# Reading an exchanged buffer back in halves, on alternate partitions and earlier

## The chip, the core and the metric

The kernel runs on one core of one Trainium2 chip. The metric is the device time of one execution in microseconds (us), lower is better. A run is "fast" or "slow" (a slow run shows a lower granted TensorE clock, or is more than 1.5% above the fastest run of the same kernel).

## The reference

Two frequency-domain filters of one input are mixed by a gate (cut to what matters; the second filter has the same form):

```python
def filt(x, w_r, w_i):                       # x: 1 x 2048 x 1024, bf16
    X = jnp.fft.rfft2(x.astype(jnp.float32), axes=(-2, -1))
    X = X * (w_r + 1j * w_i)
    return jnp.fft.irfft2(X, s=(2048, 1024), axes=(-2, -1)).astype(jnp.bfloat16)

g = sigmoid((x * gate_w).sum(-1, keepdims=True))
return g * filt(x, A_w_r, A_w_i) + (1 - g) * filt(x, B_w_r, B_w_i)
```

## The kernel before

All transforms are matmuls. The middle of the kernel goes through 16 **units** of rows, 8 for the even columns and 8 for the odd ones. Each unit is multiplied by the weights and given a first inverse transform; the result has to change its layout, so it is stored to a scratch tensor in DRAM and read back in 8 **parts** per parity. A part then gets its second inverse (L564), its third (L580 and L589), and the sums of even and odd results that make the output.

The whole program is one list of tokens. Each engine takes its own tokens in that order, and all the DMAs concerned are issued from SyncE, one in-order queue: in SyncE's timelines they come in the order of the list. The tokens that matter here:

```python
ORDER = """ ...
... EX:0:0:A H:11:1 L:0:5 VC:0:1:0:A EQ:0:0:0:P ...
... VC:0:2:1:D V:0:5:0:6 L:0:6 C:0:2:0:7 EQ:3:0:0:P L:0:7 ...
... L:1:0 EX:5:0:D C:0:4:1:6 L:1:1 EQ:3:1:0:P EX:5:1:A L:1:2 L:1:3 ...
... """
# J first inverse of a unit   R its copy out of PSUM   H its store to scratch
# L:parity:part  read-back    V second inverse         VC its copy
# C, U third inverse          EX copy of an even result for GpSimd
# EQ:part:s:h:P  one even sum on GpSimd     OC OP OR QD QP  odd sums     S store of the output
# GW gate weights   W, c loads of weights and constants   P weight product
```

The tiles and the functions that the argument touches:

```python
Re = big.tile([P, NS1 * 1024], BF16, name="re")      # even read-back (and, earlier, the input)
Ro = big.tile([P, NS1 * 1024], BF16, name="ro")      # odd read-back
y  = big.tile([P, 2, 2, 2, 2 * NT, NS1, 4], BF16, name="y")
RR = [r[:].rearrange("p (v r s f) -> p v r s f", v=8, r=2, s=2) for r in (Re, Ro)]
EV = Re[:].bitcast(F32).rearrange("p (v s f) -> p v s f", s=2, v=8)   # even sums, in the bytes of Re
# ... cut ...
def exchange_row(t, i):
    return 8 * t + 4 * (i % 2) + i // 2

def scratch_store(n, tt, q="S"):
    a = 4 * (n % NU) + 2 * tt
    Q[q].dma_start(SC[n // NU][a:a + 2].rearrange("a p m -> p a m"), RLs[n][:, tt])

def scratch_load(par, v, q="S"):
    Q[q].dma_start((Re, Ro)[par][:, v * 2048:v * 2048 + 2048],
                   SC[par][:].rearrange("a (h v q) m -> (a h) v (q m)", h=4, v=8)[:, v])

def even_mix(v, s, h, e):
    t = TM["X", v, s]
    Q[e].tensor_tensor(EV[:, v, s, 256 * h:256 * h + 256], t[:, 0], t[:, 1], (ALU.add, ALU.subtract)[h])

def store(q, v, s="b"):
    r = slice(0, 2) if s == "b" else slice(int(s), int(s) + 1)
    Q[q].dma_start(ov[:, 2 * v:2 * v + 2, :][:, r], OT[v][:, r].rearrange("p s h d -> p s (h d)"))
```

One line will matter more than it seems to: `EV`, the place of the even sums, is the tile `Re` under another type. The sums of part v go into exactly the bytes that the read-back of part v had filled, after these were used. Nobody writes waits by hand: a layer records which tile region each instruction reads and writes, and puts the semaphore waits into the built program.

## Time and profile before

| | before |
|---|---|
| time, median of 3 runs | 116.65 us (115.95 to 117.53) |
| the profiled execution | 117.98 us, span 116.2 us |
| TensorE, VectorE, ScalarE, GpSimd busy | 88%, 83%, 74%, 40% |
| last unit's matmuls end | 78.26 us |
| first odd second-inverse group starts | 90.31 us |
| GpSimd's even sums start | 74.86 us |

The profiled execution was 1.3 us longer than the median. Spans of single profiled executions therefore carry a spread of a microsecond or two; ratios come from the timed rounds.

Three views of the end. First, two rows of the stretches table (window, length, then busy us and count of TensorE, its weight loads, VectorE, ScalarE, GpSimd, then granted clock, DMA share, GB/s):

```profile
85.00:90.00 5.00, 4.05 (x52) 3.32 (x51) 1.69 (x3) 3.15 (x6) 5.00 (x8) 1.00 0.78 246
90.00:95.00 5.00, 5.00 (x59) 3.76 (x57) 3.09 (x6) 2.86 (x6) 4.53 (x7) 1.00 1.02 405
```

TensorE is four fifths busy in the first and full in the second; GpSimd is full. Next, SyncE's timeline (start, length, line, operation, out<-in, count), which shows when loads are issued:

```profile
80.66 1.31 SPq L553 DMA_DIRECT2D re<-sc  x2
85.01 5.63 SPq L553 DMA_DIRECT2D ro<-sc  x7
```

The last two even loads need 1.31 us of the queue, and seven of the eight odd loads follow from 85.01. Last, the row of the odd read-back tile (shortest/mean/longest ns, then from when to when):

```profile
L564 PE MATMUL ps<-ea,ro x64: 219/219/220, 90.3 to 108.2; 128*128 128x128 bf16 x64
```

### The profile page before, as it was taken

What the parts mean: (1) busy time and instruction counts of PE and PEld (TensorE: products, weight loads), DVE (VectorE), ACT (ScalarE), POOL (GpSimd) and SP (SyncE); (2) the same over time, 40 slices, a digit from 0 to 9 for tenths busy, and PEclk for the clock granted to TensorE, in tenths of its full rate; (3) what the DMA queues carried; (4) which work ended last, traced back from release to release, by engine and by line L of the source; (5) the groups of instructions that cost most, each with busy time, mean ns of one, the idle gap of its engine ahead of it and who ended that gap; (6) DMA issues with size and microseconds to landing.
All of it is one profiled execution on the core that took longest, in us unless ns stands there. A gap on an engine that the chain in (4) does not pass through costs nothing.

```text
span 116.2 us, 3965 instructions
## 1 busy us (share of the span) xinstructions
PE 101.9 (88%) x1619; PEld 69.5 (60%) x1619; DVE 96.0 (83%) x161; ACT 85.8 (74%) x142; POOL 46.2 (40%) x72
## 2 busy tenths in 40 slices
...
GB/s 88 295 344 406 413 367 318 367 402 393 95 202 349 367 394 393 350 395 353 254 328 302 256 281 395 379 378 379 339 266 278 402 409 148 309 261 392 80 337 205
DMA packets 17794, 36.79 MB, mean 317 GB/s; under 512 B 1904, under 2 KB 10736, under 8 KB 17776
## 3 DMA queue, kind: packets, MB, share of 16 engines
...
q14 instruction: 6, 0.05, 0.1%
...
## 4 chain that ended last, share of the span: by engine, by line
DMA 33%; PE 29%; ACT 19%; DVE 7%; SPq 4%; issue 4%; DVEq 1%; ACTq 0%
DMA re<-sc 9%; PE ps L564 9%; ACT rl L203 8%; PE ps L580 7%; DMA wj<-cst_wj 7%; DMA re<-in_x_dram 7%; DMA ro<-in_we_dram 6%; PE ps L589 5%; ACT X L203 4%; PE ps L536 4%; DMA sc<-rl 4%; ACT T L203 4%; DVE p L493 3%; DVE ot L634 3%; PE ps L449 2%
## 5 line engine op out<-in xcount | busy, mean ns | idle before, releaser
L614 POOL TENSOR_TENSOR re<-wx 128x256 f32<-128x256 f32 x24 | 17.1, 739 | 55.1 <-DMA sc<-rl 50.5
L203 ACT CAST rl<-ps 128x1024 bf16<-128x1024 f32 x28 | 28.9, 1170 | 0.2 <-PE ps L536 0.2
L203 ACT COPY wx<-ps 128x256 f32<-128x256 f32 (+1 forms) x42 | 17.8, 481 | 10.0 <-PE ps L333 6.7
L381 DVE TENSOR_TENSOR y<-ps,wx 128x256 bf16<-128x256 f32 x48 | 16.4, 412 | 7.9 <-ACT wx L203 7.8
L203 ACT CAST V<-ps 128x512 bf16<-128x512 f32 x21 | 12.3, 611 | 11.5 <-PE ps L564 8.6
L536 PE MATMUL ps<-p,wj 32*64 32x512 bf16 x512 | 19.2, 381 | 1.0 <-ACT rl L203 0.5
L493 DVE TENSOR_TENSOR p<-X,ro 128x2048 bf16<-128x2048 bf16 x16 | 18.9, 1216 | 0.0
L449 PE MATMUL ps<-fd,y 128*128 128x256 bf16 x128 | 17.3, 273 | 0.3 <-ACT ea L433 0.3
L333 PE MATMUL ps<-f,re 128*128 128x128 bf16 x256 | 15.6, 220 | 1.5 <-DMA re<-in_x_dram 1.2
L333 PEld LDWEIGHTS <-re 128*128 128x128 bf16 x256 | 14.7, 98 | 3.0 <-DMA re<-in_x_dram 2.3
L203 ACT CAST T<-ps 128x512 bf16<-128x512 f32 x26 | 16.0, 687 | 0.0
L203 ACT CAST X<-ps 128x1024 bf16<-128x1024 f32 x14 | 15.8, 1126 | 0.1
L634 DVE TENSOR_TENSOR ot<-re,ps 128x512 bf16<-128x512 f32 x20 | 12.4, 678 | 1.9 <-issue 1.9
L449 PEld LDWEIGHTS <-y 128*128 128x128 bf16 x128 | 11.1, 97 | 4.5 <-issue 3.5
L536 PEld LDWEIGHTS <-wj 32*64 32x64 bf16 x512 | 8.4, 103 | 8.1 <-issue 5.0
L381 POOL TENSOR_TENSOR y<-wx 128x256 bf16<-128x256 f32 x16 | 11.1, 736 | 5.2 <-ACT wx L203 5.2
L580 PE MATMUL ps<-ig,V 128*128 128x512 bf16 x48 | 11.5, 380 | 0.3 <-ACT V L203 0.3
L479 PE MATMUL ps<-T,wf 64*64 64x512 bf16 (+1 forms) x128 | 10.5, 333 | 1.0 <-ACT X L203 0.4
L589 PE MATMUL ps<-ig,V 128*128 128x256 bf16 x80 | 10.5, 273 | 0.3 <-ACT V L203 0.3
L205 DVE CAST V<-ps 128x512 bf16<-128x512 f32 x11 | 7.4, 683 | 3.9 <-PE ps L564 3.9
L564 PE MATMUL ps<-ea,re 128*128 128x128 bf16 x64 | 8.3, 220 | 1.9 <-DMA re<-sc 1.6
L646 POOL TENSOR_TENSOR ot<-pq 128x512 bf16<-128x512 f32 x8 | 9.9, 1268 | 0.2 <-POOL re L614 0.2
...
## 6 DMA issues: line engine op xcount, KB each, us to landing
...
```

Of the source, the lines that this page charges most:

```text
L203: nc.scalar.copy(out=out, in_=in_)
L333: nc.tensor.matmul(o, lhsT=lh, rhs=rh, start=(h == 0), stop=(h == 1))
L381: Q[e].tensor_tensor(yo[:, v, k:k + n, s1, :], a.rearrange("p (k c) -> p k c", c=4), b.rearrange("p (k c) -> p k c", c=4), op)
L449: nc.tensor.matmul(ps[:, v * 256:v * 256 + 256], lhsT=y[:, v, par, b, 2 * t:2 * t + 2, :, :].rearrange("p j s c -> p (j s c)"), rhs=C["FD" ...
L479: nc.tensor.matmul(view(ps[ho, tt * 512:(tt + 1) * 512], dst), lhsT=lh, rhs=view(T[hp(jh), tt, :], src), start=(w == 0), stop=(w == 1))
L493: nc.vector.tensor_tensor(p[:, r], xb, w, ALU.mult)
L536: nc.tensor.matmul(o, lhsT=lh, rhs=src[r, ri, wi, tt], start=(q == 0), stop=(q == 3))
L564: nc.tensor.matmul(ps[:, ch * 128:ch * 128 + 128], lhsT=RR[par][:, v, ch // 2, s, c0 + 256 * ab:c0 + 256 * ab + 128], rhs=Ew[:, s1, :], st ...
L580: nc.tensor.matmul(ps, lhsT=Vs[par, v][:, s, ch, :], rhs=rh, start=(ch == 0), stop=(ch == 3))
L589: nc.tensor.matmul(ps[:, o:o + 256], lhsT=Vs[par, v][:, s, ch, :], rhs=g[:, o:o + 256], start=(ch % 2 == 0), stop=(ch % 2 == 1))
L614: Q[e].tensor_tensor(EV[:, v, s, 256 * h:256 * h + 256], t[:, 0], t[:, 1], (ALU.add, ALU.subtract)[h])
L634: nc.vector.tensor_tensor(otile(v)[:, s, h, :], EV[:, v, s], PS["O", 1, v, s], (ALU.add, ALU.subtract)[h])
```

## The change

The intent: let the read-back of a parity begin when half of its units are stored. Each load is cut in two: half g = 0 takes the scratch rows of the parity's first four units, half g = 1 those of the other four. The rows are permuted (in `exchange_row`, through the constants) so that a half lands on every second partition instead of on 64 adjacent ones. The list of tokens was arranged anew around this, with first halves ahead of the stores of later units, and the last two output stores are cut in halves. The core of the diff (most of the list, the unpacking of arguments and a load of a constant in two pieces are cut):

```diff
 def exchange_row(t, i):
-    return 8 * t + 4 * (i % 2) + i // 2
+    r = 8 * t + 4 * (i % 2) + i // 2
+    return 2 * (r % 64) + r // 64
@@
-    def scratch_load(par, v, q="S"):
-        Q[q].dma_start((Re, Ro)[par][:, v * 2048:v * 2048 + 2048],
-                       SC[par][:].rearrange("a (h v q) m -> (a h) v (q m)", h=4, v=8)[:, v])
+    def scratch_load(par, v, g, q="S"):
+        Q[q].dma_start((Re, Ro)[par][g:P:2, v * 2048:v * 2048 + 2048],
+                       SC[par][16 * g:16 * g + 16].rearrange("a (h v q) m -> (a h) v (q m)", h=4, v=8)[:, v])
@@
-    def store(q, v, s="b"):
+    def store(q, v, s="b", h="b"):
@@
+        if h == "b":
+            Q[q].dma_start(o.rearrange("p s h d -> p s (h d)"), OT[v][:, r].rearrange("p s h d -> p s (h d)"))
+        else:
+            Q[q].dma_start(o[:, :, int(h)], OT[v][:, r, int(h)])
@@ ORDER, the stretch that matters
+... C:0:1:0:7 EX:1:1:A V:0:0:1:4 R:14:0:A R:14:1:D EQ:1:1:0:P ... EQ:1:1:1:P H:14:1 J:15:2:0
+... EX:0:1:D C:0:3:0:3 H:15:1 V:0:2:0:0 L:0:6:1 EX:3:1:D EQ:0:1:0:P V:0:5:1:1 L:0:7:0 ...
+C:0:2:1:2 EQ:3:1:0:P L:0:7:1 EX:3:0:D V:0:5:0:6 L:1:0:0 EQ:0:1:1:P C:0:2:0:0 L:1:1:0 ...
```

More of the change, by code (lines that the diff above doesn't have):

```diff
@@ L24 @@
 ORDER = """
-warm:8 c:A:F1 c:A:gws tab:A x:S:0:1 x:S:1:1 x:S:2:2 x:S:4:2 x:S:6:2 x:S:8:2 x:S:10:2 x:S:12:2 x:S:14:2 gc:P c:S:FD:0:1
-F1:1:o:0 F1:0:o:1 F1:1:e:2 F1:0:e:3 FC:1:e:A F1:3:e:4 FD:1:e FC:0:e:A F1:3:o:5 FD:0:e F1:2:e:6 FX:3:o:A FC:2:e:A
-FP:3:o FX:0:o:A F1:5:e:5 FD:2:e FC:3:e:A F1:4:e:7 FD:3:e F1:5:o:1 FC:4:e:A FP:0:o F1:4:o:6 FC:5:e:A F1:7:e:4 FD:5:e
-F1:6:e:2 FD:4:e FC:7:e:A c:S:WF:0:4 F1:9:e:3 FC:6:e:A W:S:0 F1:8:e:5 FD:6:e FC:9:e:A F1:2:o:7 FX:1:o:A FD:9:e
-c:S:WJ:0:4 F1:10:e:2 FX:4:o:A FP:1:o F1:11:e:0 FD:7:e c:S:w0 FC:8:e:A F1:6:o:3 c:S:PM FD:8:e FC:11:e:A F1:7:o:4 c:S:EZ
@@ L30 @@
-FC:10:e:A FP:4:o FX:6:o:A FD:11:e F1:12:e:6 W:S:1 F1:13:e:5 FD:10:e FC:12:e:A c:S:WF:4:16 F1:15:e:0 FX:2:o:A FP:6:o
-FD:12:e F1:14:e:3 FC:13:e:A FC:15:e:A W:S:2 F1:12:o:2 FD:13:e F1:8:o:6 FP:2:o FC:12:o:A FD:15:e F1:11:o:7 FC:14:e:A
-FX:5:o:A c:S:WJ:4:16 F1:10:o:5 FD:14:e FC:8:o:A F1:13:o:0 FP:5:o FC:10:o:A FD:12:o F1:15:o:1 neg:A:0:4 FX:7:o:A
-F2:0:0:3 FD:10:o c:S:E FC:11:o:A F2:1:1:2 W:S:3 FC:13:o:A FP:7:o FD:11:o T:0:0:A F1:9:o:4 F2:0:1:5 FC:15:o:A FD:8:o
-W:S:4 FC:9:o:A F2:1:0:3 T:0:1:A pw:P FD:13:o F1:14:o:7 T:1:0:A F3:0:5 FD:15:o c:S:FD:1:2 FC:14:o:A F2:2:1:0 X:0:A
@@ L35 @@
-T:1:1:D W:S:5 F2:2:0:3 FD:9:o F3:1:1 neg:A:4:16 F2:3:0:5 FD:14:o W:S:6 T:2:0:A F2:3:1:4 P:0:0 T:3:0:A Y:0:6 GH:3 X:1:A
-NA:0:D P:0:1 T:2:1:A T:3:1:A F3:2:0 N:0:D GC:A P:1:0 J:0:4:6 X:2:A F2:4:0:2 P:1:1 R:0:0:A Y:1:3 F2:4:1:0 GT:0:1 NA:1:D
-R:0:1:A T:4:0:D F3:3:4 Y:2:3 P:2:0 GT:2:1 T:4:1:A H:0:1 F2:5:0:2 W:S:7 X:3:A GT:3:1 c:S:IG GT:1:1 N:1:D P:2:1 F2:5:1:0
-T:5:0:A F3:4:4 GK:A T:5:1:A W:S:8 J:1:6:1 NA:2:D P:3:0 X:4:A H:0:0 F2:6:0:0 R:1:0:A W:S:9 P:3:1 F3:5:4 F2:6:1:3
-R:1:1:A H:1:0 Y:4:6 Y:3:7 P:4:0 X:5:A H:1:1 GZ:0:1 W:S:10 P:4:1 GS:0 GZ:1:4 NA:3:D GS:1 N:2:D F2:7:1:1 NA:4:D GW:D:0
@@ L40 @@
-F2:7:0:2 N:3:D J:2:6:4 N:4:D T:7:0:D T:7:1:A T:6:0:A W:S:11 T:6:1:A GW:D:4 R:2:0:A J:3:0:2 P:5:0 R:2:1:A H:2:0 F3:6:6
-P:5:1 R:3:0:A Y:5:4 F2:8:0:5 X:6:D R:3:1:A H:3:0 F3:7:0 W:S:12 H:2:1 T:8:0:A NA:5:D P:6:0 J:4:2:6 W:S:13 X:7:A P:6:1
-R:4:0:A Y:7:0 Y:6:1 F2:9:1:4 F2:8:1:5 R:4:1:A H:4:0 N:5:D NA:6:D NA:7:D W:S:14 F2:9:0:2 P:7:0 H:3:1 T:8:1:A J:5:0:6
-T:9:0:A P:7:1 T:9:1:A F3:8:2 R:5:0:A F2:10:1:5 N:7:D X:8:D F2:10:0:4 R:5:1:A H:5:0 F3:9:0 H:4:1 T:10:0:A T:10:1:D
-H:5:1 J:7:2:6 X:9:A N:6:D P:8:0 R:7:0:A J:6:4:0 P:8:1 R:7:1:A F2:11:1:2 F2:11:0:3 R:6:0:A R:6:1:D H:7:1 F3:10:6 P:9:0
@@ L45 @@
-T:11:0:A H:6:1 J:8:0:4 H:6:0 X:10:A H:7:0 T:11:1:D F2:12:0:3 R:8:0:A P:9:1 F3:11:6 R:8:1:A F2:12:1:2 H:8:0 T:12:0:D
-X:11:A H:8:1 J:9:0:4 P:10:0 W:S:15 T:12:1:A P:10:1 R:9:0:A F3:12:2 F2:13:1:6 R:9:1:A H:9:0 F2:13:0:7 P:11:0 T:13:0:A
-H:9:1 J:10:0:4 L:0:0 P:11:1 X:12:A L:0:1 L:0:2 T:13:1:A P:12:0 R:10:0:A F3:13:2 F2:15:0:6 R:10:1:D X:13:A H:10:0
-F2:14:1:7 L:0:3 F2:14:0:0 L:0:4 T:15:0:A P:12:1 J:11:2:4 T:14:0:A T:14:1:A P:13:0 R:11:0:A J:12:0:6 P:13:1 R:11:1:A
-F3:14:2 X:14:A V:0:0:0:4 F2:15:1:5 R:12:0:A R:12:1:D P:14:0 H:12:1 J:13:2:6 T:15:1:A H:12:0 H:10:1 VC:0:0:0:A P:14:1
@@ L50 @@
-F3:15:0 V:0:0:1:5 V:0:1:0:4 R:13:0:D R:13:1:A X:15:A H:13:1 C:0:0:0:6 V:0:1:1:7 VC:0:0:1:A P:15:0 H:13:0 J:14:0:2
-EX:0:0:A H:11:1 L:0:5 VC:0:1:0:A EQ:0:0:0:P VC:0:1:1:D R:14:0:A C:0:1:0:6 P:15:1 C:0:0:1:4 R:14:1:A C:0:1:1:5
-V:0:3:0:7 GW:D:8 EX:1:0:A H:14:1 J:15:0:2 H:14:0 EX:1:1:D VC:0:3:0:A H:11:0 GW:D:12 V:0:3:1:6 EQ:1:1:0:P R:15:0:A
-V:0:2:1:5 VC:0:3:1:D V:0:2:0:7 R:15:1:A H:15:0 EQ:0:0:1:P C:0:3:0:0 VC:0:2:0:D C:0:3:1:1 EQ:1:1:1:P EX:3:0:A H:15:1
-VC:0:2:1:D V:0:5:0:6 L:0:6 C:0:2:0:7 EQ:3:0:0:P L:0:7 EX:3:1:D C:0:2:1:0 VC:0:5:0:D EQ:1:0:0:P V:0:4:0:5 V:0:5:1:1
@@ L55 @@
-EQ:3:0:1:P VC:0:4:0:D V:0:4:1:6 VC:0:5:1:A EQ:1:0:1:P C:0:4:0:5 EX:0:1:A C:0:5:0:1 VC:0:4:1:A EQ:0:1:0:P C:0:5:1:4
-L:1:0 EX:5:0:D C:0:4:1:6 L:1:1 EQ:3:1:0:P EX:5:1:A L:1:2 L:1:3 V:0:6:1:1 EX:4:0:A EQ:3:1:1:P L:1:4 V:0:6:0:4 EX:4:1:A
-L:1:5 EQ:5:1:0:P L:1:6 VC:0:6:0:A VC:0:6:1:D V:0:7:1:5 EQ:5:1:1:P C:0:6:1:1 EQ:4:0:0:P V:0:7:0:4 C:0:6:0:6 EQ:0:1:1:P
-VC:0:7:0:D VC:0:7:1:A C:0:7:1:5 E:6:1:D V:1:0:0:2 EQ:4:1:0:P V:1:0:1:3 EX:7:1:D VC:1:0:0:A EQ:5:0:0:P C:0:7:0:1
-E:2:1:A VC:1:0:1:D U:1:0:0:2 EQ:7:1:0:P EQ:7:1:1:P V:1:1:0:0 U:1:0:1:3 EQ:5:0:1:P VC:1:1:0:A OC:0:0:A V:1:2:1:4
@@ L60 @@
-EQ:4:0:1:P E:2:0:A V:1:2:0:0 OP:0:0:0 OR:0:1:1 EX:7:0:A OR:0:1:0 U:1:1:0:2 VC:1:2:0:A VC:1:2:1:D V:1:1:1:1 E:6:0:A
-EQ:4:1:1:P OR:1:0:0 C:1:2:0:0 VC:1:1:1:A C:1:2:1:3 OP:0:0:1 QD:2:0:0 U:1:1:1:1 QD:2:1:0 EQ:7:0:0:P S:S:0 V:1:3:0:4
-L:1:7 QD:2:1:1 V:1:3:1:5 QP:2:0:0:P VC:1:3:0:A QD:2:0:1 V:1:4:0:6 VC:1:3:1:A OR:1:1:1 V:1:4:1:3 VC:1:4:0:A U:1:3:0:0
-QP:2:1:0:P OR:1:0:1 OR:1:1:0 U:1:3:1:4 VC:1:4:1:D QP:2:0:1:P S:S:1 U:1:4:0:1 OR:3:0:0 OR:3:1:0 U:1:4:1:5 QP:2:1:1:P
-OC:4:0:A OR:3:1:1 V:1:6:0:2 V:1:6:1:1 OP:4:0:0 OR:4:1:1 S:S:2 VC:1:6:0:A V:1:5:0:3 OR:3:0:1 VC:1:6:1:A C:1:6:0:2
@@ L65 @@
-OR:4:1:0 S:S:3 VC:1:5:0:A OP:4:0:1 C:1:6:1:4 QD:6:0:0 V:1:5:1:0 QD:6:1:0 U:1:5:0:1 VC:1:5:1:A EQ:7:0:1:P S:S:4
-QD:6:0:1 U:1:5:1:0 QP:6:0:0:P QD:6:1:1 OR:5:0:0 V:1:7:0:5 V:1:7:1:4 QP:6:1:0:P OR:5:0:1 VC:1:7:0:A VC:1:7:1:A OR:5:1:0
-U:1:7:0:5 OR:5:1:1 QP:6:1:1:P U:1:7:1:1 OR:7:0:0 S:S:5 OR:7:0:1 QP:6:0:1:P OR:7:1:1 S:S:7:0 OR:7:1:0 S:S:6 S:S:7:1
+warm:8 c:A:F1 tab:A x:S:0:1 x:S:1:1 x:S:2:2 x:S:4:2 x:S:6:2 x:S:8:2 x:S:10:2 x:S:12:2 x:S:14:2
+c:S:FD:0:1 F1:0:e:0 F1:1:e:1 FC:0:e:D F1:1:o:2 FC:1:e:A FD:0:e FD:1:e F1:3:e:3 F1:2:e:0 FC:3:e:A F1:3:o:1
@@ new lines @@
+FC:2:e:A F1:2:o:4 FD:2:e FX:3:o:A F1:4:e:5 FX:2:o:A FP:3:o F1:4:o:0 FX:1:o:A FC:4:e:D F1:5:o:1 FD:3:e
+F1:5:e:2 FP:2:o FD:4:e F1:6:e:4 FC:5:e:A F1:7:e:3 FX:5:o:A FD:5:e c:S:WF:0:4 F1:9:e:5 FC:7:e:A FP:1:o
+W:S:0 FC:6:e:A F1:8:e:1 FD:7:e FC:9:e:A F1:6:o:2 FC:8:e:A FD:9:e F1:7:o:6 c:S:WJ:0:4 FP:5:o FX:4:o:A
+F1:11:e:3 FD:8:e c:S:w0 FX:6:o:A F1:10:e:0 c:S:PM FD:6:e FC:11:e:A F1:0:o:1 c:S:gws FP:6:o FC:10:e:A
+FD:11:e F1:12:e:2 c:S:EZ F1:13:e:7 FD:10:e FC:12:e:A F1:14:e:3 FP:4:o FC:13:e:A FD:12:e FX:7:o:A F1:15:e:4
@@ new lines @@
+F1:9:o:0 FC:14:e:A FD:13:e F1:13:o:2 W:S:1 FP:7:o FC:9:o:A FD:14:e F1:15:o:5 c:S:WF:4:16 FC:15:e:A FC:13:o:A
+F1:11:o:6 FD:15:e FX:0:o:A F1:14:o:3 FC:11:o:A FD:9:o W:S:2 F1:8:o:1 FC:15:o:A gc:P neg:A:0:4 c:S:WJ:4:16
+F2:1:0:4 FD:13:o FC:14:o:A FC:8:o:A F2:1:1:0 c:S:E T:1:0:A FD:15:o F1:10:o:7 pw:P W:S:3 T:1:1:A
+F2:0:0:2 FD:11:o FC:10:o:A F3:1:4 T:0:0:A FD:8:o W:S:4 F1:12:o:0 X:1:A FD:14:o F2:0:1:2 F2:3:1:1
+FP:0:o FD:10:o FC:12:o:A c:S:FD:1:2 Y:1:3 T:0:1:A F2:3:0:6 FD:12:o W:S:5 neg:A:4:16 F3:0:4 NA:1:D
@@ new lines @@
+P:1:0 F2:2:0:2 T:3:0:A F2:2:1:0 X:0:A W:S:6 GH:3 P:1:1 T:2:0:A T:2:1:A W:S:7 N:1:D
+T:3:1:A P:0:0 GC:A c:S:IG P:0:1 F3:2:4 F3:3:0 X:2:A F2:5:0:2 Y:0:3 T:5:0:A J:1:6:4
+NA:0:D X:3:A P:2:0 F2:5:1:2 R:1:0:A Y:3:3 P:2:1 Y:2:0 F2:4:0:1 T:5:1:A H:1:0 GT:0:6
+T:4:0:A F2:4:1:7 NA:3:D W:S:8 N:0:D NA:2:D N:2:D R:1:1:A P:3:0 J:0:2:0 T:4:1:A H:1:1
+GT:2:6 P:3:1 R:0:0:A W:S:9 F3:4:4 GT:1:6 X:4:A R:0:1:D GT:3:6 F3:5:2 F2:6:0:7 GK:A
+X:5:A P:4:0 GZ:1:4 H:0:1 F2:7:1:6 H:0:0 GS:1 J:2:0:2 W:S:10 N:3:D P:4:1 T:6:0:A
@@ new lines @@
+GW:P:8 Y:4:4 F2:7:0:5 R:2:0:D R:2:1:A T:7:0:A GZ:0:2 NA:4:D T:7:1:A H:2:0 P:5:0 J:3:0:4
+GS:0 Y:5:6 F2:6:1:7 R:3:0:A N:4:D GW:D:4 T:6:1:A P:5:1 F3:7:2 H:3:0 X:7:A H:2:1
+F3:6:0 NA:5:D N:5:D X:6:A P:7:0 J:4:6:2 R:3:1:A F2:8:0:0 P:6:0 Y:7:1 R:4:0:A H:3:1
+Y:6:4 F2:8:1:5 W:S:11 NA:6:D NA:7:D P:6:1 T:8:0:A F2:9:0:4 H:4:0 T:8:1:A W:S:12 J:5:6:0
+R:4:1:A P:7:1 F2:9:1:5 R:5:0:A H:4:1 F3:8:2 T:9:0:D T:9:1:A X:8:D H:5:0 R:5:1:A W:S:13
+F3:9:4 F2:10:0:6 N:7:D N:6:D X:9:A P:8:0 H:5:1 J:7:0:2 L:0:0:0 T:10:0:A GW:D:0 R:7:0:A
@@ new lines @@
+J:6:4:6 P:8:1 R:7:1:A F2:10:1:0 F2:11:0:1 R:6:0:A R:6:1:D F2:11:1:2 T:11:0:A P:9:0 H:6:1 J:8:4:6
+T:10:1:A H:7:1 T:11:1:A H:6:0 F3:10:0 P:9:1 H:7:0 F2:12:1:2 W:S:14 R:8:0:D R:8:1:A X:10:A
+L:0:1:0 F3:11:6 L:0:2:0 F2:13:1:3 X:11:A H:8:1 F2:12:0:0 P:10:0 F2:13:0:1 T:12:0:A J:9:4:6 H:8:0
+P:11:0 T:13:0:A T:12:1:A T:13:1:A P:10:1 F3:12:0 R:9:0:A F2:14:0:2 F2:14:1:3 P:11:1 X:12:A H:9:0
+F3:13:4 L:0:3:0 T:14:0:D T:14:1:A W:S:15 R:9:1:A L:0:0:1 P:12:0 J:10:0:2 L:0:1:1 X:13:A H:9:1
+P:12:1 L:0:2:1 R:10:0:A J:11:6:4 L:0:3:1 P:13:0 R:10:1:A F3:14:0 L:0:4:1 R:11:0:D X:14:A H:10:1
@@ new lines @@
+F2:15:0:2 F2:15:1:3 R:11:1:A J:12:0:6 H:10:0 T:15:0:A T:15:1:D P:13:1 L:0:4:0 V:0:0:0:3 R:12:0:A V:0:1:1:2
+L:0:5:1 P:14:0 V:0:1:0:4 R:12:1:A H:11:1 F3:15:0 H:11:0 VC:0:1:0:A VC:0:1:1:D P:14:1 X:15:A L:0:5:0
+J:13:6:4 H:12:0 VC:0:0:0:A P:15:0 R:13:0:A L:0:6:0 J:14:0:2 H:12:1 P:15:1 R:13:1:A C:0:1:1:6 H:13:0
+C:0:1:0:7 EX:1:1:A V:0:0:1:4 R:14:0:A R:14:1:D EQ:1:1:0:P V:0:3:0:5 V:0:3:1:6 VC:0:3:0:D EQ:1:1:1:P H:14:1 J:15:2:0
+VC:0:3:1:A H:14:0 GW:D:12 VC:0:0:1:A H:13:1 C:0:0:0:5 R:15:0:A C:0:0:1:4 R:15:1:D C:0:3:1:6 H:15:0 V:0:2:1:2
@@ new lines @@
+EX:0:1:D C:0:3:0:3 H:15:1 V:0:2:0:0 L:0:6:1 EX:3:1:D EQ:0:1:0:P V:0:5:1:1 L:0:7:0 VC:0:2:0:D VC:0:2:1:A EX:0:0:A
+C:0:2:1:2 EQ:3:1:0:P L:0:7:1 EX:3:0:D V:0:5:0:6 L:1:0:0 EQ:0:1:1:P C:0:2:0:0 L:1:1:0 VC:0:5:0:D VC:0:5:1:A V:0:4:0:1
+EQ:3:1:1:P V:0:4:1:3 VC:0:4:0:D EQ:0:0:0:P C:0:5:1:6 VC:0:4:1:A EX:1:0:D C:0:4:0:1 EQ:3:0:0:P EX:5:1:A L:1:0:1 C:0:4:1:3
+EX:4:0:A EQ:5:1:0:P L:1:1:1 V:0:6:1:4 L:1:2:0 V:0:6:0:1 EQ:4:0:0:P L:1:2:1 C:0:5:0:5 EQ:0:0:1:P L:1:3:1 V:0:7:0:6
+VC:0:6:0:D VC:0:6:1:A E:2:0:A L:1:4:1 C:0:6:1:4 EQ:4:0:1:P VC:0:7:0:D L:1:5:1 V:0:7:1:7 EQ:3:0:1:P EX:4:1:D C:0:6:0:0
```

18 lines of the change are left out of this document (16 added, 2 removed).

## The prediction

> **What bounds the kernel now.** I read the page first, for shares; then the stretches table (busy time per engine, granted clock, DMA share, GB/s in windows), to cut the run into stages; then the chain that ended last, to see which wait decides each stage; then the timelines of the vector engine and GpSimd over the end.
>
> The page's first row only says that nothing is idle and nothing is full:
>
> ```profile
> PE 101.9 (88%) x1619; PEld 69.5 (60%) x1619; DVE 96.0 (83%) x161; ACT 85.8 (74%) x142; POOL 46.2 (40%) x72
> ```
>
> The stretches table gives each stage its own limit (columns: window, length, then busy us and count of PE, PEld, DVE, ACT, POOL, then clock, DMA share, GB/s):
>
> ```profile
> 50.00:72.00 22.00, 20.38 (x396) 11.18 (x393) 21.79 (x23) 22.00 (x30) 0.00 (x0) 1.00 0.96 316
> 78.00:88.00 10.00, 8.36 (x120) 6.83 (x104) 6.21 (x11) 5.68 (x10) 8.17 (x12) 1.00 0.95 327
> 100.00:106.00 6.00, 6.00 (x57) 4.01 (x56) 6.00 (x11) 2.25 (x6) 6.00 (x6) 1.00 0.75 293
> ```
>
> The reader is to see three regimes. From about 26 to 80 us (the middle row set stands for it), ScalarE and VectorE are both full: they evacuate PSUM and multiply by the weights, GpSimd does nothing, and TensorE follows. From 78 to 88 neither is full. From 94 on VectorE, GpSimd and TensorE are full together. The gap in the second stretch is explained by the chain (start, length, what):
>
> ```profile
> 78.29 1.94 ACT rl L203 x2
> 80.23 0.02 issue
> 80.25 0.36 SPq L548
> 80.61 0.05 issue
> 80.66 0.64 SPq L553
> 81.30 0.05 issue
> 81.35 6.70 DMA re<-sc
> 88.05 0.05 issue
> 88.10 0.62 PE ps L564 x8
> ```
>
> The last unit is copied out, its store (L548) is issued, and only behind it in the one in-order queue stand the last two even read-backs (L553, parts 6 and 7), though the even units were stored long before. The second needs 6.70 us to land because the stores of the last units are ahead of it. TensorE meets this twice:
>
> ```profile
> 81.42 0.45 PEld L564 LDWEIGHTS <-re 128*128 128x128 bf16 x8 [1.05 <-DMA re<-sc]
> 86.94 0.90 PEld L564 LDWEIGHTS <-re 128*128 128x128 bf16 x16 [1.15 <-DMA re<-sc]
> ```
>
> After 88.1 the chain is TensorE without a hole, until VectorE finishes. VectorE's timeline has, from 94.09, no more idle than 0.17 us, ending with
>
> ```profile
> 105.12 2.47 DVE L641 TENSOR_TENSOR pq<-re,ps 128x512 f32<-128x512 f32 x4
> 107.51 4.88 DVE L634 TENSOR_TENSOR ot<-re,ps 128x512 bf16<-128x512 f32 x8
> ```
>
> that is, 8 sums in 4.88 us, 0.605 us each, to 112.39; the last store takes the other 3.8 us. GpSimd's timeline is as dense: busy from 85.00 to 111.47 but for 0.64 us.
>
> [...] No half-partition transfer is in this trace. [...]
>
> **The change part by part.**
>
> *Read-back in halves.* 16 loads of 512 KB become 32 of 256 KB, the same 8.4 MB in the same 4 KB rows. A load waits only for its four units. By the new order the first even half is issued behind the store of unit 5 instead of unit 9, and 13 of the 16 even halves (3.4 MB) stand ahead of the last store, where 6 of 8 whole ones (3.1 MB) did. So hardly more bytes move early; what changes is what is left: 0.8 MB of even data behind the last store instead of 1.05. The odd halves all stand behind the last store, so their early start is not used much. Cost: 16 more issues at 0.32 to 0.47 us (shortest and median of the L553 rows), some 6 us of SyncE, which does nothing else. TensorE's part: the work between the last unit's matmuls (78.2) and 88.1 was 9 second-inverse groups (0.45 us each from 8 matmuls of L564) and 8 third-stage groups (0.44 us, L589): 4.0 + 3.5 = 7.5 us in 9.9. **The hole is 2.4 us.** In the new order, 9 third-stage and 6 second-inverse groups, 6.7 us, stand between the last unit and the first group that needs part 6, so it is needed at about 84.7; its last half should land near 83 to 85. I take the hole as closed but for 0.3 us.
>
> *New order, TensorE.* Counting groups behind the last unit's matmuls. Before: 27 x 0.445 + 16 x 0.44 + 12 x 0.87 = 29.5 us; after: 26 x 0.445 + 18 x 0.44 + 12 x 0.87 = 29.9. **Plus 0.4.** (0.87 is four 512-column matmuls of L580 in the chain.)
>
> *New order, the copies.* ScalarE and VectorE bound the time at which the last unit is reached, so I count both up to the last unit's copy. By pitch back to back: ScalarE 0.92 us per 1024 columns, 0.49 per 512, about 0.3 per 256; VectorE 1.13, 0.6 and 0.36, and 1.06 per weight product. ScalarE, before to after: 28 to 25 exchange copies (-2.8), 26 to 29 (+1.5) and 14 to 15 (+0.9), two first-stage copies fewer (-0.6), one parts copy fewer (-0.5): -1.5. VectorE: exchange copies 4 to 7 (+3.4), 6 to 3 (-1.8), 2 to 1 (-1.1), one gate-weight pair fewer, now on GpSimd (-0.9), one parts copy fewer (-0.6), two first-stage copies more (+0.7): -0.3. Two full engines that lose 1.8 us together can give at most 0.9 each; as they wait for each other through TensorE I take **0.4 us earlier**.
>
> *Front.* The gate coefficients' load leaves ScalarE's queue (0.47 us, ahead of the table load) and GpSimd's 4.1 us wait for it goes. Neither was in front of anything: the first TensorE group waited for the input, landing at 5.0, and the next at 8.1. About 0.
>
> *Constant E in two pieces* (120 and 8 rows): one issue of 0.32 us and no bytes. I see no reason in the profile for it; 0.
>
> *The end.* VectorE still has 28 sums, 28 x 0.605 = 16.9 us, from the first odd result, but the two V copies that sat among them (2 x 0.6) go to ScalarE: **-1.2** on that engine, if TensorE keeps ahead. GpSimd still has 22 even sums after the last unit at 0.69, then 4 x 1.25 and 8 x 1.24: 15.2 + 5.0 + 9.9 = 30.1 us; from about 80.0 that is 110.1, against 111.5. The last two stores become 256 KB each; the last one to be issued is now half of part 6, whose sums end on GpSimd about when VectorE ends, so the 3.8 us tail stays.
>
> *Sum.* TensorE ends at 110.68 - 2.1 (hole) + 0.4 - 0.4 = 108.6. VectorE ended 1.7 later, so 110.3. GpSimd 110.1 plus, say, 0.4 of gaps: 110.5. The later of the two, 110.5, plus 3.8 gives a span of 114.3; the time is 116.65 for a span of 116.2, so 114.75. I predict **114.8**, -1.6%.
>
> **The rivals.** (a) *GpSimd becomes the bound.* Its 30 us cannot start before the first new even parts come, and any slip of that start goes into the end one for one. For: it had 0.64 us of slack in 26 us. Against: the new order offers it work right behind the last unit. It would make 115.5 to 116. (b) *The wait moves into the middle.* Read-backs issued from about 52 us on compete with weight loads and stores in a stage where DMA is at 0.96; a late store holds its buffer (five of them) and ScalarE waits, and a late read-back's issue holds up every later issue in the queue. For: stores already took 5.1 us in the median, 9.8 at worst. Against: only 0.3 MB more move before the last store, less than 1 us of DMA. It would make 116 to 117.5. (c) *Everything tightens.* The order looks searched for as a whole; if both copying engines realise 0.9 us and the odd half also gains from earlier data, the end comes at 112.5 to 113.5. (d) *The read-back was hidden anyway*, and VectorE's 18 us from the first odd result are all that counts; then only the earlier start of that stage and the 1.2 us matter. It makes 115 as well, for another reason.
>
> **Range and chances.** Three engines are nearly tied in the last stage, so the gain is the least of three (1.4, 2.1 and 2.1 us before gaps): large gains need all of them. Two per cent is 2.33 us, just beyond my sum. The three runs before spread from 115.95 to 117.53, 1.4%. Hence 113.0 to 116.7 as range; faster by over 2% 0.40, within 0.56, slower 0.04.
>
> **What would show it.** In the changed profile: the waits of TensorE on the even read-back after the last unit are under 0.5 us together (hole closed); parts 6 and 7 land by 86; the last unit's exchange copy ends at 79 to 80.2; the first VectorE sum on the odd result starts near 93 (94.09 before) with no idle above 0.3 us afterwards; VectorE and GpSimd end within 0.5 us of each other near 110.4; and the tail is 3.8. DMA bytes stay 36.8 MB. I am wrong if the half loads run well below the whole ones' rate, if the last unit comes later than 80.2 because ScalarE waits on buffers or DMA in the middle, or if the first-stage order moves the start of the middle by more than 0.5 us either way.

## The result, and the profile after

| | before | after |
|---|---|---|
| time, median of 4 runs each | 116.86 us | 127.81 us (126.79 to 128.86) |
| ratio of fast runs | | 1.0914 (95%: 1.0799 to 1.1029) |
| profiled execution, span | 116.2 us | 125.9 us |
| last unit's matmuls end | 78.26 | 79.57 |
| first odd second-inverse group | 90.31 | 99.38 |
| GpSimd's even sums start; its idle in the last stage | 74.86; 4.8 us | 81.03; 10.4 us |
| TensorE, VectorE, GpSimd end | 110.68, 112.39, 111.47 | 119.34, 121.14, 122.71 |

A ratio is the mean time of one kernel's fast runs over that of the other's fast runs of the same rounds, so it is not quite the ratio of the medians. The change is slower by 9%, where 1.6% faster was predicted.

**Where the time went.** Cut each span at two points. Up to the end of the last unit's matmuls after has lost 1.3 us (79.57 against 78.26). From there to the first odd group it takes 19.8 us instead of 12.05: 7.8 us. From there to the end it takes 26.5 instead of 25.9: 0.6 us. The sum is 9.7 us, the difference of the spans. So the loss sits between about 80 and 100 us. The stretches table of the kernel after, to be held against the two rows shown of before:

```profile
85.00:90.00 5.00, 2.75 (x32) 2.09 (x30) 1.60 (x3) 2.15 (x4) 0.72 (x1) 1.00 0.24 76
90.00:95.00 5.00, 0.69 (x7) 0.72 (x8) 0.00 (x0) 0.59 (x1) 1.48 (x3) 0.77 0.51 151
95.00:100.00 5.00, 5.00 (x39) 3.94 (x37) 2.58 (x4) 0.58 (x1) 5.00 (x8) 0.55 0.97 306
```

From about 88 to 94 almost nothing is busy: from 90 to 95 TensorE works 0.69 of 5 us and VectorE not at all, and the DMA engines, which could be fetching the data that everyone waits for, run at 76 and 151 GB/s. Something is waiting for something. The granted clock falls to 0.77 and then to 0.55 in the stretch in which work resumes; 39 matmuls fit into 5 us where before had 59. This lies ahead of the first odd group (99.38), so it belongs to the 7.8 us and not to the last stage; its size is worked out below.

The chain that ended last, in that time (start, length, what), says what waits for what:

```profile
77.00 3.83 DMA sc<-rl
...
81.03 1.42 POOL re L626 x2
...
82.46 3.67 DMA re<-sc
...
86.27 0.73 POOL re L626
...
87.02 3.13 DMA re<-sc
...
90.28 0.73 POOL re L626
```

The first row is a store, which the profile infers as what released the first sums (the built program, below, names loads); then come sums on GpSimd, a load, one sum of 0.73 us, a load, one sum: the two alternate, and each load takes its 3 to 4 us alone. GpSimd's own timeline (the bracket is the idle time before, and what ended it) agrees:

```profile
81.03 1.41 POOL L626 TENSOR_TENSOR re<-wx 128x256 f32<-128x256 f32 x2 [39.77 <-DMA sc<-rl]
86.27 0.72 POOL L626 TENSOR_TENSOR re<-wx 128x256 f32<-128x256 f32 x1 [3.83 <-DMA re<-sc]
90.28 0.72 POOL L626 TENSOR_TENSOR re<-wx 128x256 f32<-128x256 f32 x1 [3.29 <-DMA re<-sc]
94.25 12.35 POOL L626 TENSOR_TENSOR re<-wx 128x256 f32<-128x256 f32 x18 [3.25 <-DMA re<-sc]
```

These sums read only copies in the tile `wx`. They have no use for the loads that they wait for. SyncE's timeline shows the price:

```profile
82.46 9.02 SPq L565 DMA_DIRECT2D re<-sc  x3
91.53 9.86 SPq L565 DMA_DIRECT2D ro<-sc  x15
```

Three even half loads hold the queue for 9.02 us (two whole ones took 1.31 before), and the 15 odd half loads stand behind them in the same in-order queue, though the last store had landed by about 86: by the view of DMA transfers the engines move next to nothing from there to 87 us (8 GB/s in 86 to 87). The first odd group starts 9.1 us later than before:

```profile
L576 PE MATMUL ps<-ea,ro x64: 219/219/268, 99.4 to 116.9; 128*128 128x128 bf16 x64
```

It was not the odd data that it waited for, though. TensorE's timeline has one long wait, for even data, and no gap between that and the first odd matmul. Two rows of the kernel after, then the same two of e1, the experiment below that differs from it in one line:

```profile
94.31 0.26 PE L576 MATMUL ps<-ea,re 128*128 128x128 bf16 x1 [6.56 <-DMA re<-sc]
99.38 0.27 PE L576 MATMUL ps<-ea,ro 128*128 128x128 bf16 x1
```

```profile
89.13 0.22 PE L576 MATMUL ps<-ea,re 128*128 128x128 bf16 x1 [1.49 <-DMA re<-sc]
91.77 0.22 PE L576 MATMUL ps<-ea,ro 128*128 128x128 bf16 x1
```

The same 32 matmuls lie between the two rows of a pair. They take 5.07 us in after and 2.64 us in e1; the granted clock was 0.50 there in after and 1.00 in e1. So the wait for even data comes first, and the low clock behind it adds 2.4 us.

**Why they wait.** The built program lists the semaphores of each instruction. The three loads and the first sums of the kernel after (row number, line, instruction, waits):

```
SyncE   79 L565 DMACopy re<-sc0 64x2048        [waits DMAHW4, Pool]
SyncE   80 L565 DMACopy re<-sc0 64x2048        [waits DMAHW5, Pool]
SyncE   81 L565 DMACopy re<-sc0 64x2048        [waits DMAHW6, Pool]
GpSimd  39 L626 TensorTensor re<-wx 128x256    [waits DMAHW3, 4, 2, 6, 1, 7, 0, Activation]
GpSimd  41 L626 TensorTensor re<-wx 128x256    [waits DMAHW4, DVE]
GpSimd  42 L626 TensorTensor re<-wx 128x256    [waits DMAHW5, DVE]
GpSimd  43 L626 TensorTensor re<-wx 128x256    [waits DMAHW6]
```

"Pool" is GpSimd. In the kernel before no even load waits for GpSimd. (In every kernel whose built program was looked at, the last odd load waits for an odd sum there; that one comes far later.) The sums in question are those of parts 1, 0 and 3, the loads those of parts 6 and 7: not one byte is shared. But the sums are written to `Re` under its second name, and a load onto `Re[g:P:2, ...]`, every second partition, is recorded as if it touched all of `Re`. So each such load is ordered behind every sum ahead of it in the list, and each sum behind every load ahead of it. The first sum is held in the same way: its DMA waits are all for even half loads. It starts at 81.03, in e1 at 76.86. The list has `EQ`, `L:0:6:1`, `EQ`, `L:0:7:0`, `EQ`, `L:0:7:1`, `EQ` in exactly this alternation. I call this the **false order**.

### The profile page after: what moved, and what is told of

Its sections match the earlier page's. It is cut to its first block, busy times and chain, and to the rows that moved or that the text cites. A ratio compares the mean times of both kernels' runs of the same rounds, so it can differ in the third digit from the quotient of the medians.

```text
span 125.9 us, 3992 instructions
## 1 busy us (share of the span) xinstructions
PE 104.3 (83%) x1616; PEld 72.1 (57%) x1619; DVE 97.9 (78%) x160; ACT 85.6 (68%) x141; POOL 48.3 (38%) x74
## 4 chain that ended last, share of the span: by engine, by line
DMA 29%; POOL 20%; PE 20%; ACT 12%; SPq 8%; issue 5%; DVE 2%; POOLq 1%; DVEq 0%
DMA re<-sc 12%; POOL ot L658 7%; PE ps L345 6%; POOL re L626 6%; ACT rl L212 6%; SPq L565 6%; DMA re<-in_x_dram 5%; DMA sc<-rl 5%; PE ps L461 4%; DMA y<-in_wo_dram 4%; DMA ro<-sc 4%; POOL ot L642 4%; POOL y L393 3%; PE ps L491 3%; ACT T L212 2%
## 5 line engine op out<-in xcount | busy, mean ns | idle before, releaser
L212 ACT CAST rl<-ps 128x1024 bf16<-128x1024 f32 x25 | 25.6, 1069 | 0.5 <-PE ps L548 0.5
L212 ACT CAST V<-ps 128x512 bf16<-128x512 f32 x23 | 13.0, 591 | 16.0 <-PE ps L576 15.8
L212 ACT COPY wx<-ps 128x256 f32<-128x256 f32 (+1 forms) x38 | 16.4, 481 | 7.8 <-PE ps L345 6.8
L505 DVE TENSOR_TENSOR p<-X,ro 128x2048 bf16<-128x2048 bf16 x16 | 20.0, 1277 | 0.0
L212 ACT CAST T<-ps 128x512 bf16<-128x512 f32 x29 | 16.9, 639 | 0.0
L345 PEld LDWEIGHTS <-re 128*128 128x128 bf16 x256 | 14.6, 98 | 3.1 <-DMA re<-in_x_dram 2.5
L576 PE MATMUL ps<-ea,re 128*128 128x128 bf16 x64 | 8.9, 230 | 7.9 <-DMA re<-sc 7.9
L214 DVE CAST V<-ps 128x512 bf16<-128x512 f32 x9 | 6.2, 692 | 11.0 <-PE ps L576 11.0
L576 PEld LDWEIGHTS <-re 128*128 128x128 bf16 x128 | 8.5, 103 | 9.0 <-issue 6.8
L601 PE MATMUL ps<-ig,V 128*128 128x256 bf16 x80 | 12.6, 302 | 0.0
L491 PE MATMUL ps<-T,wf 64*64 64x512 bf16 (+1 forms) x128 | 11.3, 332 | 0.6 <-ACT rl L212 0.2
```

The lines of the kernel that those rows point to most:

```text
L212: nc.scalar.copy(out=out, in_=in_)
L345: nc.tensor.matmul(o, lhsT=lh, rhs=rh, start=(h == 0), stop=(h == 1))
L491: nc.tensor.matmul(view(ps[ho, tt * 512:(tt + 1) * 512], dst), lhsT=lh, rhs=view(T[hp(jh), tt, :], src), start=(w == 0), stop=(w == 1))
L505: nc.vector.tensor_tensor(p[:, r], xb, w, ALU.mult)
L576: nc.tensor.matmul(ps[:, ch * 128:ch * 128 + 128], lhsT=RR[par][:, v, ch // 2, s, c0 + 256 * ab:c0 + 256 * ab + 128], rhs=Ew[:, s1, :], st ...
L601: nc.tensor.matmul(ps[:, o:o + 256], lhsT=Vs[par, v][:, s, ch, :], rhs=g[:, o:o + 256], start=(ch % 2 == 0), stop=(ch % 2 == 1))
```

## The experiments

Theory: the false order costs most of the 11 us (127.81 - 116.86). Rivals: (A) half loads are simply slower in transfer; (B) the new list is slower whatever the loads are; (C) the even data cannot come earlier without the odd data coming later, so the hole that the prediction wanted to close was not to be had; (D) the pair of gate weights moved to GpSimd delays the middle stage; (E) the copying engines alone set the middle stage, so that filling its dry stretches of DMA gains nothing; (F) the even data and GpSimd's sums set the end, so that an early start of the odd halves gains nothing. Runs of one group went to one chip and share its runs of the kernel before.

### First group: halves, order, aliasing

**e1_ev_elsewhere.** The kernel after, with the sums put into `y`, which is dead by then. One line; no token moves:

```diff
-    EV = Re[:].bitcast(F32).rearrange("p (v s f) -> p v s f", s=2, v=8)
+    EV = y[:].rearrange("p v e b t s c -> p (v e b t s c)").bitcast(F32).rearrange("p (v s f) -> p v s f", s=2, v=8)
```

> The changed kernel, with one line altered: GpSimd's even sums (EV) lie in the memory of y, free by then, instead of in Re, so they share no tile with the read-backs. Theory (false order: a load onto every second partition is taken to overlap all of Re, so loads and GpSimd's sums into Re wait for each other in turn): the three even loads behind the last store are issued within 2 us instead of 9.0, TensorE's hole of 7 us near 90 goes, the clock stays at 1.0, and the time falls from 127.8 to 115 to 117. Rival A (the half loads themselves are slow[...]): the loads still land late, the hole stays, 122 or more. Rival B (the new order is bad by itself): 122 or more, with the waits elsewhere.

Measured: 119.65 us against 116.48 of before, ratio 1.0188 (1.0098 to 1.0279), above the expected 115 to 117. In its built program no even load waits for GpSimd any more. SyncE's timeline and the first odd group:

```profile
81.47 1.92 SPq L565 DMA_DIRECT2D re<-sc  x3
83.44 10.60 SPq L565 DMA_DIRECT2D ro<-sc  x15
```

```profile
L576 PE MATMUL ps<-ea,ro x64: 219/219/219, 91.8 to 109.2; 128*128 128x128 bf16 x64
```

The three loads take 1.92 us of the queue instead of 9.02, and the odd half begins at 91.8 instead of 99.4. TensorE's waits for even data shrink by 4.7 us (1.49 and 0.41 instead of 6.56), and the granted clock is 1.00 in each stretch from 80 to 105, which is the 2.4 us worked out above. One line of aliasing removes some 8 of the 11 us. About 1.8% stays.

**e2_contiguous_halves.** Sums still in `Re`, but the halves on adjacent partitions, with the old `exchange_row`:

```diff
-    r = 8 * t + 4 * (i % 2) + i // 2
-    return 2 * (r % 64) + r // 64
+    return 8 * t + 4 * (i % 2) + i // 2
@@
-        Q[q].dma_start((Re, Ro)[par][g:P:2, v * 2048:v * 2048 + 2048],
+        Q[q].dma_start((Re, Ro)[par][64 * g:64 * g + 64, v * 2048:v * 2048 + 2048],
```

> The changed kernel with EV still in Re, but the halves are partitions 0 to 63 and 64 to 127 instead of alternate ones (rows of the constant put back to match). In the built program no load waits for GpSimd then. Theory: no false order, so the time falls to 115 to 118[...]. Rival A: 122 or more, worse than the run with EV elsewhere by over 4 us. Rival B: 122 or more.

Measured: 128.29 against 116.48, ratio 1.0979 (1.0904 to 1.1054). The expected time was missed by far, although the order is clean: no even load waits for GpSimd in the built program. Two rows of its stretches table, then the typical odd half load (count, KB, median us from issue to landing), here and in e1:

```profile
95.00:100.00 5.00, 3.40 (x43) 2.54 (x41) 2.24 (x4) 2.36 (x6) 3.88 (x6) 1.00 1.03 223
100.00:105.00 5.00, 4.64 (x38) 2.76 (x36) 3.04 (x6) 2.35 (x5) 5.00 (x7) 1.00 1.04 228
```

```profile
ro<-sc SPq DMA_DIRECT2D x16, 256.0 KB, 8.8
```

```profile
ro<-sc SPq DMA_DIRECT2D x16, 256.0 KB, 5.2
```

The DMA share is 1.03 while only 223 to 228 GB/s move. So for adjacent halves rival A holds, and only for them: 8.8 us instead of 5.2 to land. The permuted rows of the change avoid this: in a stretch in which only odd loads of 64 alternate partitions move, the stretches table of the kernel after has

```profile
100.00:105.00 5.00, 4.95 (x55) 3.56 (x54) 2.67 (x4) 4.59 (x9) 5.00 (x8) 1.00 0.97 379
```

379 GB/s: with alternate partitions the loads reached that rate. As a test of the false order e2 says little, since it puts one cost in the place of another.

**e3_order_alone.** The new list with the halved output stores, but whole loads at the place of the second half:

```diff
-L:0:0:0 ... L:0:0:1 ...
+... L:0:0 ...                 # the same for all 16 parts; scratch_load and exchange_row as before
```

> The new order and the halved last stores, but whole 512 KB loads on all partitions, each where its second half stood. Theory: no false order; even parts 6 and 7 land behind the last store as before, so 115 to 118. Rival A: the same, 115 to 118. Rival B (new order bad by itself): 122 or more.

Measured: 120.67 against 116.48, ratio 1.0353 (1.0303 to 1.0403), between the two expectations (115 to 118, and 122 or more). Rival B has something in it: without halves the new list costs 3.5%. The halves, once freed from the false order, take 1.6% of this back (e1).

**e4_halves_in_old_order.** The old list, each load cut into two alternate halves at the same place, sums in `Re`:

```diff
-L:0:6 ... L:0:7 ...
+L:0:6:0 L:0:6:1 ... L:0:7:0 L:0:7:1 ...
```

> The old order with each load replaced by its two strided halves, one after the other; EV in Re. Theory: the built program has two loads that wait for GpSimd and sums that wait for loads, so several us of hole near 82 to 92: 119 to 125 against 116.9 before. Rival A: slower as well, 118 or more, but with the loads landing late rather than issued late. Rival B: 116 to 117.5, no hole.

Measured: 127.5 against 116.48, ratio 1.095 (1.0899 to 1.1001); the mechanism is as expected, the size a little above the expected range. The list of what SyncE waits for (total us, times, longest):

```profile
SPq L548 <- POOL re L609: 7.0, 2, 3.6
```

Halving the loads alone, in the old list, brings the whole loss: the new list is not needed for it.

### Second group: what the halves and the list are worth without the false order

**e5_halves_no_false_order.** e4 with the sums in `y`:

```diff
-    EV = Re[:].bitcast(F32)...
+    EV = y[:]...bitcast(F32)...        # as in e1
```

> The run with halves in the old order, but with EV in the memory of y. Theory: the 11 us that halves cost in the old order were the false order alone, so 116 to 118, within 1.3% of before. Rival A (halves cost by themselves): 120 or more.

Measured: 118.59 against 116.9 as medians (its profile and one more run were slow); fast runs give 1.0053 (0.9989 to 1.0118). With e4 this is the second pair that differs in one line: 1.095 to 1.005. It also says that the halves alone gain nothing.

**e6_even_first.** e1, with the last three even halves issued right behind the first half of part 6, ahead of the last seven stores:

```diff
-... L:0:6:0 ... L:0:6:1 ... L:0:7:0 ... L:0:7:1 ...
+... L:0:6:0 L:0:6:1 L:0:7:0 L:0:7:1 ...
```

> The changed kernel with EV in y, and the last three even halves (6:1, 7:0, 7:1) issued right behind 6:0, ahead of the last stores. Theory: what is left of TensorE's hole (2.8 us of load waits at 86 and 87.5 to 89 in the run with EV elsewhere) came from their place behind the last store, so 119.65 falls by about 2 to 117 to 118. Rival C: DMA is full there, the stores and the odd loads come later by as much, and the time stays at 119 to 120.

Measured: 119.16 against 116.9, ratio 1.0181 (1.0109 to 1.0253). TensorE's two waits for even data (2.4 us in e1) are gone, but it now waits 1.7 us for the first odd data, and the DMA share is 0.59 from 85 to 90. No gain: rival C.

**e7_gate_on_vector.** e1, with the gate-weight pair back on VectorE:

```diff
-GW:P:8
+GW:D:8
```

> The changed kernel with EV in y, and the one gate-weight pair back from GpSimd to VectorE. Theory: on GpSimd it took 1.52 + 1.15 us and stretched a weight product of VectorE from 1.21 to 2.17, so moving it back costs VectorE 0.86 and gives back about 0.96: no difference, 119 to 120. Rival D: it was the start of the delay in the middle stage (the next groups also wait for it), so 118.5 or less.

Measured: 118.16 against 116.9, ratio 1.0113 (1.0049 to 1.0178). In e1 the pair falls beside a weight product of VectorE (timeline), whose longest instance differs between the two kernels (rows of the tile `ro`, e1 then e7; shortest/mean/longest ns):

```profile
39.24 1.15 POOL L451 TENSOR_TENSOR eb<-e,ea 128x512 bf16<-128x512 bf16 x1
39.30 2.17 DVE L505 TENSOR_TENSOR p<-X,ro 128x2048 bf16<-128x2048 bf16 x1
```

```profile
L505 DVE TENSOR_TENSOR p<-X,ro x16: 1214/1219/2173, 24.3 to 47.4; 128x2048 bf16<-128x2048 bf16 x16
```

```profile
L488 DVE TENSOR_TENSOR p<-X,ro x16: 1210/1217/1227, 25.0 to 48.0; 128x2048 bf16<-128x2048 bf16 x16
```

One product takes 2.17 us instead of 1.22, 0.95 us more, and it is the one that starts beside GpSimd's instruction (39.30 and 39.24); what the two share is not shown. On VectorE the two cancel: the 0.9 us of work moved off it came back as a longer product. That was the theory, and by it the time should have stayed. It fell by about 0.8 us (1.0188 to 1.0113, though the intervals overlap) and into the range of rival D. By what path the pair costs time is not shown.

**e8_old_even_first.** The kernel before, with its last two even loads issued five stores earlier:

```diff
-... L:0:5 ... L:0:6 ... L:0:7 ...
+... L:0:5 L:0:6 L:0:7 ...
```

> The kernel before, with even parts 6 and 7 (whole loads) issued right behind part 5, ahead of the last five stores. Theory (as in the prediction): the hole of 2.4 us near 81 to 88 closes and the end follows by 1 to 2 us: 114.3 to 115.7. Rival C (DMA full): the last stores, and so the odd loads, come up to 2.6 us later and the gain is eaten: 116 to 117.5.

Measured: 120.48 against 116.9, ratio 1.0306 (1.0237 to 1.0375): slower. The last store to scratch lands at 87.75 instead of 85.0, because 1 MB of loads now runs ahead of it, and all odd loads wait for it. One stretch shows it:

```profile
85.00:90.00 5.00, 4.06 (x52) 3.31 (x49) 3.10 (x5) 2.70 (x6) 5.00 (x8) 1.00 0.37 97
```

DMA moves 97 GB/s where before moved 246; then TensorE, which still waits 1.1 us for even data, waits 2.8 us for odd data; in before it had waited 2.2 us, all for even data. This is rival C in the old list: closing the hole at the even data opens a larger one at the odd data.

### Third group: dry stretches and early odd halves

**e9_fill_old.** DMA nearly stops in the kernel before from 30 to 32 us (18 GB/s). Three loads of the weights and a constant are moved up to fill it:

```diff
-... W:S:6 ... W:S:7 ... c:S:IG ... W:S:8 ...
+... W:S:6 W:S:7 c:S:IG W:S:8 ...
```

> The kernel before, with weight loads 7 and 8 and the constant IG issued ahead of the first exchange store, behind which SyncE stood from 22 to 31.9 us while DMA ran dry (share 0.05 in 30 to 32). Theory (DMA is a shared bound from 24 to 90 us): the dry stretch of some 2.6 us is filled, later loads and stores come earlier, and the time falls by 0.5 to 2 us, to 114.8 to 116.3. Rival E (the copying engines alone set the middle stage): no change, within 0.3 us.

Measured: 116.49 against 116.88, ratio 0.9967 (0.9894 to 1.0041). The stretch is filled (405 GB/s), the time is the same.

**e10_fill_new.** The like in e7:

```diff
-... W:S:9 ... W:S:10 ... W:S:11 ...
+... W:S:9 W:S:10 W:S:11 ...
```

> The new order with EV in y and the gate pair on VectorE, and weight loads 10 and 11 issued ahead of the stores of units 0 and 2 behind which they stood while DMA ran at a share of 0.34 to 0.79 in 42 to 50 us. Theory: the dry stretch shrinks by up to 2.6 us (1 MB), the first second-inverse groups no longer wait at 69 to 71, and 118.2 falls to 116.5 to 117.8. Rival E: no change, 118 to 118.5.

Measured: 119.3 against 116.88, ratio 1.0225 (1.0148 to 1.0302), not better than e7's 1.0113. The low DMA share only moved from one place to the next (0.34 at 42 to 44 us in e7; 0.54 and 0.50 at 46 to 50 here). It tells nothing else.

**e11_odd_first_halves.** e5 with the remaining loads in a row behind the last store, first odd halves early among them:

```diff
-H:11:0                                    # where it stood
+H:11:1 H:11:0
@@
+H:15:1 L:0:6:0 L:0:6:1 L:0:7:0 L:0:7:1 L:1:0:0 L:1:1:0 L:1:2:0 L:1:0:1 L:1:1:1 L:1:2:1 L:1:3:0 L:1:3:1 ...
```

> The old order with halves, EV in y, and the first halves of odd parts 0 to 2 issued right behind the even ones (they need only units 8 to 11), so that DMA does not wait idle for the last store to land; the second halves follow. Theory: DMA share in 82 to 90 rises from 0.8 to 0.95 or more, and the time is 0.5 to 1.5 us below the run with halves and no false order (118.6): 117 to 118. Rival F (the even read-backs and GpSimd's sums set the end, not the odd ones): no change.

Measured: 119.13 against 116.88, ratio 1.0213 (1.0136 to 1.0291). DMA is full from 82 to 92 us (share 1.02, 374 GB/s), as wanted, and still the first odd group starts no earlier after the last unit (13.1 us, against 12.05 in before and 13.3 in e15 below, the same kernel with the loads at their old places). No gain, as rival F expected. Its reason is not shown: TensorE still waits 1.4 us for odd data just ahead of that group.

**e12_odd_first_and_fill.** e11 with the edit of e9:

```diff
+W:S:6 W:S:7 c:S:IG W:S:8                  # on top of e11
```

> Both: first odd halves early, and the weight loads 7 and 8 and IG ahead of the first store. Theory: the gains add up, 115 to 117, the best of the kernels with halves and perhaps below the kernel before. Rivals E and F: as the run without the filling, or as before at best.

Measured: 119.21 against 116.88, ratio 1.0187 (1.0117 to 1.0257). A miss, too.

### Fourth group: the small differences again, with five rounds

The kernels of e1, e7, e5 and e9, unchanged, on one chip (before: 116.59 us):

```diff
 # e13 = e1     e14 = e7     e15 = e5     e16 = e9
```

> The changed kernel with EV in y, again, beside the next three on one chip. If the residual of the new order is real, a ratio to before of 1.012 to 1.025; if it was noise between chips, 1.00 to 1.01.

> The same with the gate pair on VectorE. If the pair on GpSimd costs what the earlier two runs differ by, 0.5 to 1.0% below the run beside it; if that was noise, the same within 0.3%.

> The old order with halves and EV in y, again. If halves are neutral where no false order arises, a ratio of 0.997 to 1.010. The difference to the run with the gate pair on VectorE is then what the rest of the new order costs: 0.5 to 1% expected, 0 if that was noise.

> The kernel before with weight loads 7, 8 and IG ahead of the first store, again, for a tighter interval: a ratio of 0.990 to 1.000; if below 0.995 with its interval under 1, it is the only version that beats both kernels.

| kernel | median us | ratio to before |
|---|---|---|
| e13: after, sums elsewhere | 118.79 | 1.0182 (1.0116 to 1.0249) |
| e14: the same, gate pair on VectorE | 118.52 | 1.0103 (1.0020 to 1.0187) |
| e15: old list, halves, sums elsewhere | 117.54 | 1.0079 (1.0016 to 1.0142) |
| e16: before, dry stretch filled | 116.74 | 1.0033 (0.9971 to 1.0095) |

The gate pair is worth about 0.7 or 0.8% in both pairs (e1 and e7, e13 and e14), though the intervals overlap each time. e16 agrees with rival E for the old list: filling the dry stretch gains nothing. That the copying engines are the reason is argued, not shown. The profiled execution of e9 had a span of 114.0 us, the shortest of all; had I gone by that one look, I would have reported a gain.

### Fifth group: another way out of the false order, and a control

**e17_loads_before_sums.** The kernel after, sums still in `Re`, but the three loads ahead of GpSimd's first sum in the list:

```diff
-... L:0:6:0 ... EQ:1:1:0:P ... EQ:1:1:1:P ... L:0:6:1 ... EQ:0:1:0:P ... L:0:7:0 ... EQ:3:1:0:P L:0:7:1 ...
+... L:0:6:0 L:0:6:1 L:0:7:0 L:0:7:1 ... EQ:1:1:0:P ... EQ:1:1:1:P ... EQ:0:1:0:P ... EQ:3:1:0:P ...
```

> The changed kernel, EV still in Re, but the three late even halves issued ahead of GpSimd's first even sum in program order. Theory (false order): loads no longer wait for sums; the sums wait once for the last of these loads, which land near 81 to 84, and run on from there, so 117 to 121 instead of 127.8, without moving EV. Rival (moving EV did something else that helped): 125 or more.

Measured: 119.11 against 116.96, ratio 1.0181 (1.0039 to 1.0323). Here the tile stays shared; only the alternation goes. GpSimd's timeline (only its order counts):

```profile
83.36 15.13 POOL L609 TENSOR_TENSOR re<-wx 128x256 f32<-128x256 f32 x22 [42.79 <-ACT V L195]
```

22 sums in one piece, without a gap. Its list is that of e6, from which it differs in the one line of `EV`, and the ratios are the same, 1.0181 each (e17's interval is the wide one). With the loads ahead of the sums, the place of the sums makes no difference. So it was not the place of the sums in memory that made e1 quick: the order alone was the cost.

**e18_old_ev_elsewhere.** The control: the kernel before with the sums in `y`:

```diff
-    EV = Re[:].bitcast(F32)...
+    EV = y[:]...bitcast(F32)...        # as in e1, on the kernel before
```

> Control: the kernel before with EV in y. Theory: nothing changes, 0.995 to 1.005 of before, as no load is halved. If it costs 0.5% or more, the cost that the halves show without false order (1.005 and 1.008) is that of moving EV, not of the halves.

Measured: 116.35 against 116.96, ratio 0.9958 (0.9837 to 1.0079). Moving the sums by itself changes nothing measurable.

No version beats the kernel before clearly: e9, e16 and e18 are the same within their intervals.

## Why the prediction was wrong, point by point

- **The step that failed: "A load waits only for its four units."** The three loads of parts 6 and 7 waited for GpSimd's sums, 7.7 us in all by SyncE's waits of the kernel after, and the sums waited 10.4 us for loads, the late start of the first not counted. I read the waits off the algorithm and off the bytes. They come from what is recorded, and a load onto every second partition was recorded as touching the whole tile. Two pairs that differ in one line (after and e1; e4 and e5), the reordering e17 (beside e6) and the control e18 show it.
- **"I take the hole as closed but for 0.3 us."** It became a wait of 6.6 us for even data, which ended at 94.3, and the clock of 0.50 behind it cost 2.4 us more. But the step would have failed without the false order too: e1's fast runs (117.99 and 119.42) still lie outside the predicted 113.0 to 116.7. In e1 TensorE still waits (counted at its weight loads) 0.7 us before 86.1 and 1.7 before 89.1, as much together as the hole of 2.4 us of before, and part 7 lands at 89.0, not by 86. In e6, where the even data does come in time, and in e8, where the later of the two waits for it closes, a wait turns up at the odd data (1.7 and 2.8 us). The even hole and the start of the odd loads hang on the same stores; I priced one and left out the other.
- **"0.4 us earlier" for the last unit.** Its matmuls end 1.3 us later in after and 0.6 later in e1. Of the gains counted for the copying engines, the 0.9 us for the gate pair was undone by the 0.95 us that the pair cost VectorE (e7), which I had not looked for.
- **The half loads' rate.** This doubt of mine was unfounded: 64 alternate partitions reached 379 GB/s, 5.5 us from issue to landing in the median (6.6 for a whole load of twice the size before). Adjacent halves failed in e2: 223 to 228 GB/s, 8.8 us to land. The price of an issue was too low: 0.32 to 0.47 us was taken, and the odd half loads took 0.59 in the median. What that costs in time was not tested.
- **The end.** "VectorE and GpSimd end within 0.5 us of each other near 110.4": 121.14 and 122.71. The last stage itself was about right: from the first odd group to the end 25.8 to 26.1 us in before and in every kernel from e5 to e12, and in e1 and e3; 26.5 in after, 26.7 in e17 (a slow profile), 27.1 in e4, 28.4 in e2. So in these **the start of that group decides** the end, and nothing that I gained behind it (1.2 us of copies moved off VectorE, halved last stores) showed.
- **The rivals.** Rival (a) came near: GpSimd's start slips, its next 18 even sums started at 94.25, and it had no gap from there to 122.7. But such a slip does not go in one for one: in e17 the first sum starts 6.5 us later than in e1 (83.36, in a slow profile), and the fast runs are as quick. Rival (b) had the other half, that "a late read-back's issue holds up every later issue in the queue", but looked for it in the middle. Both were priced at about a microsecond, since I took the waits as small. "Slower" got 0.04; it should have been much more for a change that puts new loads among the writes of an aliased tile.
- **What stays open.** Without the false order 1.8% remains. By e13 to e15 about half or less is the halves (0.8%, whose interval reaches down to 0.2%) and 0.8% the gate pair; the intervals are too wide to add these up. Why the new list costs 3.5% with whole loads (e3) beyond the gate pair and the late place of those loads is not settled.
